# Loads, hashes and splits of the first two head pairs put in another order, and a ranking with its offset summed by TensorE

## The chip, the cores and the metric

The kernel runs on one core of one Trainium2 chip. Its engines are TensorE (PE; its weight loads stand apart as PEld), VectorE (DVE), ScalarE (ACT), GpSimd (POOL) and SyncE (SP), which here only issues DMAs. The metric is the device time of one execution in microseconds, and less is better. Before the change the median of three executions was 389.96 us (389.85 to 390.24).

## The reference

Two stages follow one another. The first is attention on 4 batches of 8 heads, 768 positions of 64 numbers, in which a query sees only keys of its own hash bucket; the bucket is the six signs of a projection.

```python
q_bits = (np.einsum('bhsd,dk->bhsk', q, proj) > 0).astype(np.int64)
q_bucket = np.sum(q_bits * powers, axis=-1)           # k likewise
mask = q_bucket[:, :, :, None] == k_bucket[:, :, None, :]
scores = np.where(mask, scale * np.matmul(q, k.transpose(0, 1, 3, 2)), -1000000000.0)
attn = softmax(scores)                                # + 1e-9 in the divisor
return np.matmul(attn, v)
```

The second takes each batch's 768 x 512 result x, scores each token with `x @ w_gate`, picks the 128 best tokens and adds to them the output of a two-layer ReLU network (512 to 1024 to 512), times the sigmoid of the score.

## The kernel before

**Units.** A head is the unit. Heads are counted 0 to 31; all but head 0 come in pairs that share one load X (128 partitions: two heads of 64 numbers, 768 positions), once for queries (r = 0) and once for keys (r = 1). Head 0 has its own load, Xa, in four pieces, and its own code (the functions with `first` in their names). Exact products are made from two 16-bit parts: a high part that ScalarE rounds (`split_xh`, L495) and a low part, the rest, by VectorE (`split_xl`, L502). V is split the same way (L550, L556).

**What a head needs.** Its projected signs are hashed on TensorE (L463), turned into bits of weight 2^13 on VectorE (`signs`, L480), and its parts and bits are copied to their partitions by DMAs of SP: tile A holds bits and high parts, tile B the low parts (`place_*`, L509). Then come:

- the row maxima over the keys of the same bucket: 6 blocks of two matmuls (`max_unit`, L671), for each a ReLU on ScalarE (tile me, L679) and a reduction on VectorE (tile mj, L688), which gives M. M is turned and put back into A as one more row. A trick halves the columns: the first matmul takes the difference of two halves (`k_diff` L661/L663, `diff_first`);
- nine score blocks of 512 columns (`st_unit`, L722 and L726, tile st) and their exponentials on ScalarE (`st_exp`, L740/L742, tile P);
- the rest R of each exponential beyond bf16, by VectorE (L757) or, for some chunks, by GpSimd (L760), and the product with V (`av`, L776);
- reciprocals and products on VectorE (`recip`, `norm`).

**Beside it.** Weights of the network are loaded and split (`weights`); scores of the finished heads are summed on VectorE (`score`, L813: part 0 over the first 256 columns, part 1 over the rest); batches 0 to 2 are ranked and run through the network while later heads compute (`choose`, `apply_expert`, `expert_steps`). Batch 3 is ranked last (`rank_last`): a token's rank is a count of larger scores, made by VectorE's comparisons (`compare`) and by TensorE's sums of columns (`count`); `pick` makes 128 x 128 selection matrices sel from the ranks, and TensorE uses them to gather (L1177).

**What sets the order.** Every step is an event with a number; the table ORDER says in which sequence the 2676 steps are written down, and each engine executes its own instructions in that sequence, waiting for what its operands need. SP's DMAs are a queue too. PSUM banks are handed out in the order of the table (four for maxima and odd jobs, three for st, one for av), and tiles with a tag have a fixed number of buffers. `mine` remembers a VectorE instruction and `turn` makes the next GpSimd operation wait for it, so that the two do not work on SBUF at once. `keep_warm` writes matmuls of ones into a spare bank (tile wq, L311); nobody reads them.

Of the kernel before, what the change touches and what calls it, by code (L numbers as in the profile page):

```python
# [20 lines left out]
P = 128  # L21
# [222 lines left out]
def body(ctx, tc, qk, v, pj, wg, w1, w2, cst, out):  # L244
# [92 lines left out]
    w1l = cp.tile([P, 4, FF], BF16, name="w1l")  # L337
    w2h = cp.tile([P, 8, DM], F16, name="w2h")
    w2l = cp.tile([P, 8, DM], BF16, name="w2l")

    def load_consts():
        nc.sync.dma_start(cs, cst)

# [3 lines left out]
    def make_ident():  # L347
        nc.scalar.copy(ident16, ident)
# [780 lines left out]
    def rank_last(b):  # L1129
# [39 lines left out]
        for t in range(NC):  # L1169
            pick(sel, t, rank)  # L1170
# [197 lines left out]
```

## Time and profile before

| | |
|---|---|
| median of three executions | 389.96 us |
| profiled execution | 389.61 us |
| its span (first to last instruction) | 387.5 us |
| around the span | 2.11 us |
| busy share PE / DVE / ACT / POOL | 97 / 89 / 81 / 47% |
| granted TensorE clock, mean | 0.99 |

Busy shares are means over the whole span. In the page's 40 slices PE has 6, 8 and 8 tenths in the first three and 9 or more from the fourth to the last but one. [...] A row of a timeline is: start in us, time in us, engine, line, operation, output<-input, shapes, and in brackets how long the engine had been idle and what ended that. [...]

### The profile page before, as it was taken

What the parts mean: (1) busy time and instruction counts of PE and PEld (TensorE: products, weight loads), DVE (VectorE), ACT (ScalarE), POOL (GpSimd) and SP (SyncE); (2) the same over time, 40 slices, a digit from 0 to 9 for tenths busy, and PEclk for the clock granted to TensorE, in tenths of its full rate; (3) what the DMA queues carried; (4) which work ended last, traced back from release to release, by engine and by line L of the source; (5) the groups of instructions that cost most, each with busy time, mean ns of one, the idle gap of its engine ahead of it and who ended that gap; (6) DMA issues with size and microseconds to landing.
All of it is one profiled execution on the core that took longest, in us unless ns stands there. A gap on an engine that the chain in (4) does not pass through costs nothing.

```text
span 387.5 us, 14129 instructions
## 1 busy us (share of the span) xinstructions
PE 374.8 (97%) x5728; PEld 272.6 (70%) x5738; DVE 345.9 (89%) x935; ACT 313.3 (81%) x665; POOL 181.2 (47%) x103
## 2 busy tenths in 40 slices
PE   6889999999999999999999999999999999999995
PEld 4346777677676777687657877667677788778794
DVE  3889999999899989999999999999999999999842
ACT  7899999899998988988588888988988995774210
POOL 8135567474647275655335362545236352630113
PEclk9799999999999999999999999999999999999999
DMA  7568677677776475565855552756463524010301
GB/s 243 148 193 232 172 199 232 169 203 177 223 209 181 100 214 125 140 188 150 208 136 157 135 155 61 217 161 177 100 178 103 113 58 125 6 38 3 110 29 56
DMA packets 26353, 56.37 MB, mean 145 GB/s; under 512 B 4218, under 2 KB 10942, under 8 KB 26288
## 3 DMA queue, kind: packets, MB, share of 16 engines
q1 hardware_dynamic: 15936, 36.92, 36.6%
q10 hardware_dynamic: 9680, 16.45, 13.5%
q0 software_dynamic: 672, 2.10, 1.7%
q8 instruction: 45, 0.74, 0.8%
q14 instruction: 20, 0.16, 0.2%
HBM read 26.58 MB, written 7.35 MB: 88 GB/s over the span
## 4 chain that ended last, share of the span: by engine, by line
PE 78%; issue 7%; ACT 5%; DVE 5%; DMA 2%; POOL 1%; POOLq 0%; SPq 0%; ACTq 0%; DVEq 0%
PE av L776 24%; PE bank L671 14%; PE st L722 14%; PE st L726 14%; PE bank L463 3%; PE bank L995 3%; PE bank L1019 2%; DMA A<-sg 2%; DVE R L757 2%; ACT me L679 1%; ACT P L740 1%; DMA Xa<-in_qk_dram 1%; DVE mj L688 1%; DVE jks L813 1%; PE bank L598 1%
## 5 line engine op out<-in xcount | busy, mean ns | idle before, releaser
L760 POOL TENSOR_TENSOR R<-P 128x1536 f16<-128x1536 f32 x46 | 133.8, 2910 | 134.4 <-DVE V L556 21.1
L776 PEld LDWEIGHTS <-P 128*128 128x128 bf16 x2304 | 125.8, 98 | 26.7 <-issue 1.3
L776 PE MATMUL av<-V,P 128*128 128x65 f16 (+2 forms) x2304 | 133.3, 193 | 0.1
L776 PE MATMUL av<-V,R 128*128 128x65 f16 (+1 forms) x1152 | 126.4, 193 | 0.0
L740 ACT ACTIVATE P<-st 128x512 f32<-128x512 f32 x192 | 111.9, 598 | 17.7 <-PE av L776 9.7
L722 PE MATMUL st<-A 128*128 128x512 f16 (+1 forms) x384 | 119.3, 326 | 1.4 <-ACT P L740 1.2
L726 PE MATMUL st<-B 128*128 128x512 f16 (+1 forms) x384 | 118.6, 326 | 0.7 <-ACT B L432 0.7
L688 DVE CUSTOM_DVE_ANT_0 mj<-bank,me 128x384 bf16<-128x384 f32 x192 | 102.2, 550 | 15.6 <-ACT me L679 7.4
L671 PE MATMUL bank<-A 128*128 128x384 f16 x384 | 108.4, 329 | 3.8 <-DVE A L410 1.0
L776 PEld LDWEIGHTS <-R 128*128 128x128 f16 x1152 | 105.9, 97 | 0.1
L679 ACT ACTIVATE me<-bank 128x384 f32<-128x384 f32 x192 | 92.4, 491 | 14.8 <-PE bank L671 5.7
L757 DVE TENSOR_TENSOR R<-P 128x768 f16<-128x768 f32 x100 | 96.8, 987 | 0.4 <-ACT P L740 0.2
L742 ACT ACTIVATE P<-st 128x512 f32<-128x512 f32 x96 | 56.9, 596 | 2.2 <-PE st L726 0.7
L671 PEld LDWEIGHTS <-A 128*128 128x128 f16 x384 | 34.8, 98 | 23.1 <-issue 4.8
L726 PEld LDWEIGHTS <-B 128*128 128x128 f16 x384 | 37.5, 98 | 18.0 <-issue 2.5
L722 PEld LDWEIGHTS <-A 128*128 128x128 f16 x384 | 37.4, 97 | 15.8 <-issue 2.5
L502 DVE SCALAR_TENSOR_TENSOR T<-X,T 128x768 f16<-128x768 f32 x32 | 31.4, 992 | 0.0
L495 ACT ACTIVATE T<-X 128x768 f16<-128x768 f32 x32 | 26.6, 841 | 0.4 <-DMA B<-T 0.4
L837 POOL TENSOR_TENSOR w1l<-W,w1h 128x512 bf16<-128x512 f32 x8 | 12.8, 1604 | 13.6 <-DVE M L688 4.9
L837 POOL TENSOR_TENSOR w2l<-W,w2h 128x512 bf16<-128x512 f32 x8 | 12.3, 1545 | 12.5 <-DVE R L757 4.0
L798 DVE TENSOR_TENSOR x<-av,rc 128x384 f32<-128x384 f32 x32 | 17.7, 553 | 0.2
L995 PEld LDWEIGHTS <-w1h 128*128 128x128 f16 x256 | 15.9, 98 | 2.1
(137 smaller groups left out, 409.5 us busy)
## 6 DMA issues: line engine op xcount, KB each, us to landing
X<-in_qk_dram SPq DMA_DIRECT2D x32, 384.0 KB
B<-T SPq DMA_DIRECT2D x62, 192.0 KB
A<-T SPq DMA_DIRECT2D x31, 240.0 KB
V<-in_v_dram ACTq DMA_DIRECT2D x16, 384.0 KB
out_dram<-x ACTq DMA_DIRECT2D x6, 768.0 KB
W<-in_w_dram ACTq DMA_DIRECT2D x8, 512.0 KB
sbc<-scores SPq DMA_DIRECT2D x3, 384.0 KB
A<-sg SPq DMA_DIRECT2D x31, 31.5 KB
```

Of the source, the lines that this page charges most:

```text
L502: mine(nc.vector.scalar_tensor_tensor(t[:, o : o + S], st["X", p, r], XS, t[:, i : i + S], op0=ALU.mult, op1=ALU.subtract))
L671: nc.tensor.matmul(pt[:, :384], a[0][:, t * P : (t + 1) * P], a[1][:, 384:768] if i else K[h % NA], start=True, stop=True,)
L679: nc.scalar.activation(me, st["mx", h, t, 0][:, :384], AF.Relu)
L688: nc.vector.tensor_tensor_reduce(out=jk, in0=st["mx", h, t, 1][:, :384], in1=st["me", h, t], op0=ALU.add, op1=ALU.max, scale=1.0 / MS, sca ...
L722: nc.tensor.matmul(pt[:, o : o + n], a[1][:, c * P : (c + 1) * P], a[0][:, q0 : q0 + n], start=True, stop=False,)
L726: nc.tensor.matmul(pt[:, o : o + n], bt[:, 0, c * P : (c + 1) * P], bt[:, 1, q0 : q0 + n], start=False, stop=True,)
L740: nc.scalar.activation(pp[:, r, 0:512], pt, AF.Exp, scale=ES)
L742: nc.scalar.activation(pp[:, :, 512:768], pt.rearrange("p (a b) -> p a b", a=2), AF.Exp, scale=ES)
L757: mine(nc.vector.tensor_tensor(t[:, r], pp[:, r], hi_view(pp, r), op=ALU.subtract))
L760: turn(nc.gpsimd.tensor_tensor(t, pp, hi_view(pp, a), op=ALU.subtract))
L776: nc.tensor.matmul(o[:, t, :n], l, vv[:, c, hh, v0 : v0 + n], start=False, stop=last and l is lo, skip_group_check=True,)
L995: nc.tensor.matmul(hp[:, f * P : (f + 1) * P], w[:, k, o : o + P], x[:, k * P : (k + 1) * P], start=(f == 0 and k == 0 and i == order[0]), ...
```

## The change

Six things change.

- **Loads.** In the first microseconds SP loads only head 0 (Xa), pair 0 (X0_0, X0_1) and the 128 x 128 identity. V0, X1_1 and X1_0 get a wait for VectorE's last sign instruction of head 0 (`gate`). The rest of the constants (`cs`) also has it and stands later. V0 is issued by SP and no longer by ScalarE.
- **Hashes of pairs 0 and 1.** They were hashed together, each half of the columns in one PSUM bank. Now each pair has its bank, 64 partitions of it used twice (`hash_pair`), and `sign_pair` makes two sign instructions and one difference per pair on VectorE. Before, the difference of this first group was GpSimd's.
- **High parts.** X0_1's and X1_0's are made by GpSimd (`tensor_scalar`) instead of ScalarE. The 16-bit identity is cast by VectorE instead of ScalarE.
- **Order.** The first 300 events of ORDER stand in another sequence; some 25 of the later ones move by a few places, at most some dozen (steps of `choose` and `apply`, a `split_xl` and a `max_red`). Two `keep_warm` of eight matmuls each move from within head 0's maxima to within head 2's.
- **Scores.** Part 1's instructions are remembered by `mine`, so the GpSimd operation written next waits for them.
- **Ranking.** For batch 3 `behind` adds one matmul of the identity with six columns of constants to the count, and sel is then made by one comparison instead of a subtraction and a comparison.

```diff
--- before.py
+++ after.py
@@ -53,160 +53,160 @@
 ORDER = (
-    0, 142, 288, 289, 20, 15, 1, 16, 11, 21, 72, 144, 7, 75, 83, 141, 77, 10, 76, 85, 6, 71, 24, 12,
...
+    0, 10, 20, 9, 6, 142, 144, 146, 143, 59, 1, 21, 27, 15, 16, 3, 17, 18, 7, 72, 74, 76, 73, 12,
...
@@ -338,14 +338,17 @@
     w2h = cp.tile([P, 8, DM], F16, name="w2h")
     w2l = cp.tile([P, 8, DM], BF16, name="w2l")
 
+    def load_ident():
+        nc.sync.dma_start(cs[:, :P], cst[:, :P])
+
     def load_consts():
-        nc.sync.dma_start(cs, cst)
+        behind_of(nc.sync.dma_start(cs[:, P:], cst[:, P:]), "gate", "load")
 
     def load_gate():
         nc.scalar.dma_start(wgt, wg)
 
     def make_ident():
-        nc.scalar.copy(ident16, ident)
+        nc.vector.tensor_copy(ident16, ident)
 
     def make_consts():
         nc.vector.tensor_copy(iota16, iota)
@@ -359,13 +362,17 @@
     def mine(i):
         st["port"] = i
 
+    def behind_of(i, key, why):
+        if key in st:
+            tc.add_manual_dep(
+                getattr(i, "ins", i), getattr(st[key], "ins", st[key]).name,
+                mybir.DependencyInfo(mybir.DependencyClass.Sync, mybir.DependencyReason.SCHED_ONLY),
+                reason=why,
+            )
+
     def turn(i):
-        if TURNS and "port" in st:
-            tc.add_manual_dep(
-                getattr(i, "ins", i), getattr(st["port"], "ins", st["port"]).name,
-                mybir.DependencyInfo(mybir.DependencyClass.Sync, mybir.DependencyReason.SCHED_ONLY),
-                reason="port",
-            )
+        if TURNS:
+            behind_of(i, "port", "port")
 
     def need(*keys):
 
@@ -375,12 +382,16 @@
 
     def load_x(p, r):
         x = sb.tile([P, S], F32, tag="X", name=f"X{p}_{r}", bufs=XB)
-        nc.sync.dma_start(x, qk[p, r])
+        i = nc.sync.dma_start(x, qk[p, r])
+        if p == 1:
+            behind_of(i, "gate", "load")
         st["X", p, r] = x
 
     def load_v(pr):
         t = sb.tile([P, NC, 2, D], F32, tag="V", name=f"V{pr}", bufs=1)
-        (nc.scalar if ACT_V else nc.sync).dma_start(t, v[pr])
+        i = (nc.scalar if pr else nc.sync).dma_start(t, v[pr])
+        if not pr:
+            behind_of(i, "gate", "load")
         st["V", pr] = t
 
     def negate():
@@ -407,7 +418,7 @@
         j, n = 32 * (2 * e + r), 2 * NB + 2
         x, y = st["hpa", r, e][j : j + n, :384], A[0][r][0:n, e * 384 : (e + 1) * 384]
         if r:
-            nc.vector.tensor_scalar(
+            st["gate"] = nc.vector.tensor_scalar(
                 y, x, pjt[j : j + n, 64:65], pjt[j : j + n, 65:66], op0=ALU.is_gt, op1=ALU.mult
             )
         else:
@@ -454,6 +465,32 @@
         nc.scalar.copy(A[0][0][0:1, t0 * P : t1 * P], pt[0:1, :n])
         pmax.give(f"mt0_{e}")
         st[("row1", 0) if e else ("row", 0)] = True
+
+    def hash_pair(p):
+        hp = st["hpp", p] = pmax.take(f"hpp{p}")
+        for e in range(2):
+            for r in range(2):
+                i = 64 * e + 32 * r
+                nc.tensor.matmul(
+                    hp[i : i + 32, :384], pjt[:, 0:32], st["X", p, r][:, e * 384 : (e + 1) * 384],
+                    start=True, stop=True, tile_position=(0, i),
+                )
+
+    def sign_pair(p):
+        if ("sg", 0) not in st:
+            st["sg", 0] = sb.tile([P, S // 2 + S], F16, tag="sg", name="sg0", bufs=2)
+        w = slice(64 * p, 64 * p + 64)
+        hp, t = st["hpp", p], st["sg", 0][w]
+        sd, sg = t[:, : S // 2], t[:, S // 2 :]
+        for e in range(2):
+            i = slice(64 * e, 64 * e + 64)
+            nc.vector.tensor_scalar(
+                sg[:, e * 384 : (e + 1) * 384], hp[i, :384], pjt[i, 66:67], pjt[i, 67:68],
+                op0=ALU.is_gt, op1=ALU.mult,
+            )
+            st["sgd", p, e] = True
+        pmax.give(f"hpp{p}")
+        mine(nc.vector.tensor_tensor(sd, sg[:, 0:384], sg[:, 384:768], op=ALU.subtract))
 
     def hash_half(g, e):
         hp = pmax.take(f"hp{g}_{e}")
@@ -483,16 +520,16 @@
         )
         pmax.give(f"hp{g}_{e}")
         if e:
-            if g:
-                mine(nc.vector.tensor_tensor(sd, sg[:, 0:384], sg[:, 384:768], op=ALU.subtract))
-            else:
-                nc.gpsimd.tensor_tensor(sd, sg[:, 0:384], sg[:, 384:768], op=ALU.subtract)
+            mine(nc.vector.tensor_tensor(sd, sg[:, 0:384], sg[:, 384:768], op=ALU.subtract))
 
     def split_xh(p, r):
         if ("T", p) not in st:
             st["T", p] = sb.tile([P, TW], F16, tag="T", name=f"T{p}", bufs=TB)
         o = KH if r else QH
-        nc.scalar.activation(st["T", p][:, o : o + S], st["X", p, r], AF.Copy, scale=XS)
+        if (p, r) not in {(0,1),(1,0)}:
+            nc.scalar.activation(st["T", p][:, o : o + S], st["X", p, r], AF.Copy, scale=XS)
+        else:
+            nc.gpsimd.tensor_scalar(st["T", p][:, o : o + S], st["X", p, r], XS, None, op0=ALU.mult)
         st["XH", p, r] = True
 
     def split_xl(p, r):
@@ -810,12 +847,14 @@
         for t in range(t0, t1):
             st["scd", b, part, t] = True
             jk = sb.tile([P, 384], BF16, tag="jks", name=f"jks{b}_{part}_{t}", bufs=2)
-            nc.vector.tensor_tensor_reduce(
+            i = nc.vector.tensor_tensor_reduce(
                 out=jk[:, : d1 - d0], in0=x[:, t, d0:d1], in1=wgt[:, d0:d1],
                 op0=ALU.mult, op1=ALU.add, scale=1.0,
                 scalar=st["sc", b, part - 1][:, t : t + 1] if part else 0.0,
                 accum_out=sc[:, t : t + 1],
             )
+            if part:
+                mine(i)
 
 
     def load_w(i):
@@ -861,10 +900,15 @@
             op1=ALU.mult, accum_out=cnt[:, i : i + 1],
         ))
 
-    def count(i, cm, rp):
+    def behind(rp):
+        nc.tensor.matmul(
+            rp[:, :NC], ident, cs[:, 3 * P + NC : 3 * P + 2 * NC], start=True, stop=False, skip_group_check=True
+        )
+
+    def count(i, cm, rp, first=True):
         for j in range(i, NC):
             nc.tensor.matmul(
-                rp[:, j : j + 1], cm[:, j], oneb[:, 0:1], start=(i == j == NC - 1), stop=(i == 0),
+                rp[:, j : j + 1], cm[:, j], oneb[:, 0:1], start=first and i == j == NC - 1, stop=(i == 0),
                 skip_group_check=True,
             )
 
@@ -1151,6 +1195,7 @@
                     bp[:, j0 * P : j1 * P],
                 )
         rp = st_bank(f"rp{b}")
+        behind(rp)
         yield
         cnt = sb.tile([P, NC], F32, tag="cnt", name=f"cnt{b}", bufs=1)
         cms = {}
@@ -1159,15 +1204,15 @@
             compare(i, sc, sbc, cms[i], cnt)
             yield
             if i < NC - 1:
-                count(i + 1, cms[i + 1], rp)
+                count(i + 1, cms[i + 1], rp, False)
                 yield
-        count(0, cms[0], rp)
+        count(0, cms[0], rp, False)
         yield
         rank = sb.tile([P, NC], F32, tag="rank", name=f"rank{b}", bufs=1)
         nc.vector.tensor_tensor(rank, rp[:, :NC], cnt, op=ALU.subtract)
         sel = sb.tile([P, NC, P], F16, tag="T", name=f"sel{b}", bufs=TB)
         for t in range(NC):
-            pick(sel, t, rank)
+            nc.vector.tensor_scalar(sel[:, t], iota16, rank[:, t : t + 1], None, op0=ALU.is_equal)
         yield
         need(*(("xsl", k) for k in range(4)))
         xs, xps = st["xs"], [mx_bank(f"xp{b}_{r}") for r in range(2)]
@@ -1240,10 +1285,14 @@
     at(low_first, 0)
     for i, n in enumerate(WARM[2:]):
         at(keep_warm, 2 + i, n)
-    for g in range(NH // 4):
+    for p in range(2):
+        at(hash_pair, p)
+        at(sign_pair, p)
+    for g in range(1, NH // 4):
         for e in range(2):
             at(hash_half, g, e)
             at(signs, g, e)
+    at(load_ident)
     for fn in (score_v, score_vh, score_vl):
         at(fn)
     for k in range(4):
```

Numbers behind a name in the rows that follow are the head or pair, the part and the buffer: `X0_1` is pair 0's keys, `me0_3` the ReLU of head 0's block 3, `T0` pair 0's high and low parts, `sg0` the signs of pairs 0 and 1.

On ACT, from the end of Xa's high parts on, there stands before:

```order
L415 ACTIVATE s00_170<-bank0_64,pjt_75 14x384
L416 ACTIVATE A0_90<-s00_170,pjt_75 14x384
L415 ACTIVATE s01_175<-bank2_66,pjt_75 14x384
L416 ACTIVATE A0_90<-s01_175,pjt_75 14x384
L495 ACTIVATE T0_182<-X0_1_163 128x768
L679 ACTIVATE me0_1_189<-bank0_64 128x384
L679 ACTIVATE me0_3_194<-bank2_66 128x384
L679 ACTIVATE me0_0_228<-bank0_64 128x384
L383 DMA V0_230<-in_v_dram 128x768
L495 ACTIVATE T1_235<-X1_0_165 128x768
L495 ACTIVATE T1_235<-X1_1_167 128x768
L495 ACTIVATE T0_182<-X0_0_187 128x768
```

and with the change:

```order
L530 ACTIVATE T0_185<-X0_0_183 128x768
L426 ACTIVATE s00_198<-bank0_64,pjt_75 14x384
L427 ACTIVATE A0_90<-s00_198,pjt_75 14x384
L426 ACTIVATE s01_201<-bank2_66,pjt_75 14x384
L427 ACTIVATE A0_90<-s01_201,pjt_75 14x384
L443 ACTIVATE B0_94<-Xa_105 64x768
L716 ACTIVATE me0_0_209<-bank3_67 128x384
L716 ACTIVATE me0_1_216<-bank0_64 128x384
L443 ACTIVATE B0_94<-Xa_105 128x768
L716 ACTIVATE me0_2_237<-bank0_64 128x384
L716 ACTIVATE me0_3_240<-bank1_65 128x384
L587 ACTIVATE V0_96<-V0_214 128x12x64
```

X0_0's high part now stands ahead of head 0's signs, and head 0's two parts of B (L443) among its first maxima; X0_1's, X1_0's and the identity's casts are gone, X1_1's stands five rows below the end of the piece, and the load of V0 has left this queue.

On DVE, from the first instruction that waits for Xa, there stands before:

```order
L438 SCALAR_TENSOR_TENSOR B0_94<-Xa_105,A0_90 64x768
L410 TENSOR_SCALAR A0_90<-bank1_65,pjt_75 14x384
L410 TENSOR_SCALAR A0_90<-bank3_67,pjt_75 14x384
L422 TENSOR_TENSOR A0_90<-A0_90 128x384
L688 ISA mj0_1_225,M0_84<-bank3_67,me0_1_189 128x384
L688 ISA M0_84 128x1
L688 ISA mj0_3_232,M0_84<-bank2_66,me0_3_194 128x384
L688 ISA M0_84 128x1
L688 ISA mj0_0_252,M0_84<-bank1_65,me0_0_228 128x384
L688 ISA M0_84 128x1
```

and with the change:

```order
L449 SCALAR_TENSOR_TENSOR B0_94<-Xa_105,A0_90 64x768
L421 TENSOR_SCALAR A0_90<-bank1_65,pjt_75 14x384
L539 SCALAR_TENSOR_TENSOR T0_185<-X0_0_183,T0_185 128x768
L421 TENSOR_SCALAR A0_90<-bank3_67,pjt_75 14x384
L351 CAST ident16_87<-cs_74 128x128
L433 TENSOR_TENSOR A0_90<-A0_90 128x384
L487 TENSOR_SCALAR sg0_219<-bank1_65,pjt_75 64x384 x2
L493 TENSOR_TENSOR sg0_219<-sg0_219 64x384
L725 ISA mj0_0_223,M0_84<-bank2_66,me0_0_209 128x384
L725 ISA M0_84 128x1
```

X0_0's low part now stands between the two sign instructions of head 0 (L421), the second of which is the gate; the identity and pair 0's signs and difference follow ahead of the first reduction.

On SP, behind the first two loads, there stands before:

```order
L378 DMA X0_1_163<-in_qk_dram 128x768
L378 DMA X1_0_165<-in_qk_dram 128x768
L378 DMA X1_1_167<-in_qk_dram 128x768
L378 DMA X0_0_187<-in_qk_dram 128x768
L302 DMA Xa_105<-in_qk_dram 64x768
L342 DMA cs_74<-in_cst_dram 128x397
L302 DMA Xa_105<-in_qk_dram 64x768
L509 DMA A1_91<-T0_182 64x1920
L378 DMA X2_1_262<-in_qk_dram 128x768
L509 DMA A1_91<-sg0_260 14x1152
L509 DMA A1_91<-sg0_260 14x768
```

and with the change:

```order
L385 DMA X0_0_183<-in_qk_dram 128x768
L385 DMA X0_1_188<-in_qk_dram 128x768
L342 DMA cs_74<-in_cst_dram 128x128
L302 DMA Xa_105<-in_qk_dram 64x768 x2
L392 DMA V0_214<-in_v_dram 128x768
L385 DMA X1_1_229<-in_qk_dram 128x768
L385 DMA X1_0_232<-in_qk_dram 128x768
L546 DMA A1_91<-T0_185 64x1920
L546 DMA A1_91<-sg0_219 14x1152
L546 DMA A1_91<-sg0_219 14x768
L546 DMA A2_92<-T0_185 64x1920
```

Pair 0 and the identity come first and Xa's upper halves right behind them; V0, X1_1 and X1_0 stand behind these and ahead of the first copy to A1, and the wait of the gate is V0's.

## Rows read from the trace of the kernel before

**Rows 1.** Stretches: us, busy us and count per engine, PE clock, DMA share, GB/s.

```profile
8.00:15.70 7.70, 6.90 (x43) 2.85 (x43) 4.77 (x13) 6.62 (x13) 2.96 (x4) 0.56 0.74 192
15.70:20.00 4.30, 3.09 (x18) 1.23 (x17) 4.30 (x8) 3.69 (x8) 0.24 (x1) 1.00 0.49 144
20.00:24.00 4.00, 2.96 (x17) 1.53 (x16) 3.27 (x12) 3.47 (x9) 1.03 (x1) 1.00 0.95 273
24.00:28.00 4.00, 3.73 (x35) 1.96 (x34) 3.46 (x12) 4.00 (x11) 2.18 (x2) 1.00 0.54 150
28.00:46.00 18.00, 17.92 (x293) 12.62 (x292) 17.25 (x43) 17.65 (x39) 10.59 (x6) 1.00 0.68 192
46.00:360.00 314.00, 311.69 (x4994) 228.94 (x4999) 296.33 (x807) 268.19 (x574) 151.26 (x61) 1.00 0.53 145
```

**Rows 2.** Chain of waits, first 60 us: start us, us, what ended last.

```profile
0.75 3.28 DMA Xa<-in_qk_dram
...
9.99 0.85 PE wq L311 x8
...
11.49 2.71 PE bank L463 x16
...
39.91 1.43 PE bank L463 x16
```

**Rows 3.** Timeline of ACT, first 20 us: start us, us, line, tiles.

```profile
4.05 1.59 ACT L392 ACTIVATE A<-Xa 64x768 f16<-64x768 f32 x2 [1.11 <-DMA Xa<-in_qk_dram]
5.76 0.57 ACT L415 ACTIVATE s<-bank,pjt 14x384 f32<-14x384 f32 x1
...
7.60 0.61 ACT L416 ACTIVATE A<-s,pjt 14x384 f16<-14x384 f32 x1
...
8.97 0.87 ACT L679 ACTIVATE me<-bank 128x384 f32<-128x384 f32 x2
...
10.69 2.31 ACT L495 ACTIVATE T<-X 128x768 f16<-128x768 f32 x3
...
18.22 0.60 ACT L740 ACTIVATE P<-st 128x512 f32<-128x512 f32 x1 [0.48 <-PE st L726]
```

**Rows 4.** Timeline of DVE, first 20 us.

```profile
4.92 0.95 DVE L438 SCALAR_TENSOR_TENSOR B<-Xa,A 64x768 f16<-64x768 f32 x1 [3.02 <-ACT A L392]
5.91 1.39 DVE L410 TENSOR_SCALAR A<-bank,pjt 14x384 f16<-14x384 f32 x2
...
15.34 1.41 DVE L438 SCALAR_TENSOR_TENSOR B<-Xa,B 64x768 f16<-64x768 f32 x1
```

**Rows 5.** Groups by line and form: count, busy us, mean ns.

```profile
L760 POOL TENSOR_TENSOR R<-P 128x1536 f16<-128x1536 f32 x46 | 133.8, 2910 | 134.4 <-DVE V L556 21.1 <-DVE R L757 20.3 <-ACT me L679 12.6
...
L837 POOL TENSOR_TENSOR w1l<-W,w1h 128x512 bf16<-128x512 f32 x8 | 12.8, 1604 | 13.6 <-DVE M L688 4.9 <-ACT w1h L835 2.5 <-ACT me L679 1.9
...
L480 DVE TENSOR_SCALAR sg<-bank,pjt 128x384 f16<-128x384 f32 x16 | 10.5, 672 | 0.8 <-PE bank L463 0.6
...
L813 DVE CUSTOM_DVE_ANT_0 jks<-x,wgt,sc 128x256 bf16<-128x256 f32 x18 | 7.7, 477 | 0.0
...
L661 DVE TENSOR_TENSOR T<-T 128x384 f16<-128x384 f16 x15 | 5.7, 381 | 0.0
```

**Rows 6.** Timeline, first 20 us: the DMA queue of SP, POOL and PE.

```profile
1.81 2.12 SPq L378 DMA_DIRECT2D X<-in_qk_dram  x4
...
15.03 0.91 POOL L489 TENSOR_TENSOR sg<-sg 128x384 f16<-128x384 f16 x1 [4.59 <-DVE sg L480]
...
15.97 1.77 SPq L509 DMA_DIRECT2D A<-sg  x2
...
19.14 0.65 PE L671 MATMUL bank<-A 128*128 128x384 f16 x3 [0.22 <-DMA A<-sg]
```

**Rows 7.** Timeline of the last ranking, 365 to 372 us.

```profile
367.89 1.43 DVE L874 TENSOR_SCALAR sel<-iota,cs,rank 128x128 f16<-128x128 f16 x6
...
368.79 2.84 PE L1177 MATMUL bank<-sel,xs 128*128 128x128 f16 x48
```

306 rows, old and new, of the table ORDER are left out of this document.

## The prediction, made before the changed kernel had run

> **What bounds the kernel now.** I read four views, in this order: the busy slices of the page, the table by stretches, the chain of waits of the first 60 us, and the timelines of ACT and DVE there. In the slices the reader is to see that PE is full from the fourth slice on. The stretches put numbers to it [rows 1]: from 28 to 46 us PE is idle for 0.08 of 18 us and from 46 to 360 us for 2.3 of 314. What is gained there must be PE's own work, and the change takes none away. Before 28 us it is another kernel: from 15.7 to 24 us PE idles 1.21 + 1.04 = 2.25 us, and from 8 to 15.7 us it has 43 matmuls, at a clock of 0.56. There the chain runs through the first loads, ACT and DVE. ACT idles 1.08 + 0.61 + 0.53 = 2.22 us between 8 and 24 us, DVE 2.93 + 0 + 0.73 + 0.54 = 4.20 us between 8 and 28 [rows 1]. The first exponential, from which all heads follow, starts at 18.22 us [rows 3]. So the question is how much sooner the start hands a full queue to PE, and whether ACT and DVE, 85% and 94% busy in the long stretch (268.19 and 296.33 of 314), can then keep that lead.
>
> **Loads and head 0.** A load lands 3.28 us after its issue when nothing is ahead of it [rows 2]. SP issues four X from 1.81 us in 2.12 us, 0.53 each [rows 6]. X0_0 now has the first of these places, behind Xa's pieces, and I put its landing at 6.4 us: 1.81 + 3.28, and 1.3 for the bytes ahead of it (an estimate; 5.1 without them is the lower bound). On ACT it stands ahead of head 0's signs. ACT ends Xa's high parts at 4.05 + 1.59 = 5.64 us [rows 3], waits 0.75 us, and splits X0_0 in 0.77 us (three in 2.31 [rows 3]), to 7.2. The four sign instructions took from 5.76 to 8.21 us, 2.45 in all [rows 3], and now end at 9.6. DVE does X0_0's low part (0.95, as the 768 columns of B [rows 4]) between its two signs (1.39 for two [rows 4]): it starts when ACT has the high part, at 7.2, and the gate falls at 7.2 + 0.95 + 0.70, about 8.9, instead of 5.91 + 1.39 = 7.3. Both engines' bits, which the maxima need, are there 1.4 to 1.6 us later than before.
>
> It is made good in what follows. On ACT from 9.6, with 0.77 us for each cast of 768 columns and 0.87 for two me [rows 3]: one part of B to 10.4, me0_0 and me0_1 to 11.2, the other part of B to 12.0, two me to 12.9, V0's high part to 13.6 (V0 is issued at 8.9 and lands by 12.3 if it takes the 3.28; cover 0.6 us), the issue of a weight load, at SP's 0.53, to 14.2, two me to 15.0, the row's cast, at a sign's 0.6, to 15.6, X1_1's high part to 16.4. Nothing in this list waits for a landing later than 12.3 or for GpSimd. The first exponential then starts at 16.2 to 16.6 us, against 18.22: 1.6 to 2.0 us sooner, and I take **1.8**. Head 1's tile A is sooner too: its signs are on DVE by 11.2 us; two such copies are 1.77 us of SP's time, and PE waited for the second until 19.14, 3.2 after their first issue at 15.97 [rows 6]; that gives 14.4 now, ahead of need.
>
> **GpSimd's two high parts.** No row has a GpSimd operation of this form. From below: R's pace, 2910 ns for 1536 columns, is 1.9 ns a column, 1.46 us for 768, and with one input less perhaps half, 0.75; from above: w1l's pace, 1604 ns for 512, gives 2.4 us [rows 5]. I take 1.5. X0_1's starts at about 7.5 us, when X0_1 has landed one place behind X0_0, and feeds a difference, head 1's tile A and a low part that DVE reaches at 12.2; even 2.4 us is hidden. X1_0's has from 14 to 20 us. ACT loses 2 x 0.77 = 1.54 us of work and the identity's cast, 0.13 or more at the same pace per column: about 1.7.
>
> [...]
>
> **Sign work on DVE.** A sign instruction costs by its columns and not its partitions: 0.70 us for 14 partitions [rows 4], 0.672 for 128 [rows 5]. Two become four for pairs 0 and 1, +1.34 us; two differences come from GpSimd, 2 x 0.38 [rows 5] = 0.76; the identity's cast is some 0.15. DVE has **2.25 us more** to do before head 1 is through. It has 4.20 us of idle time to put it in. By the steps above I see it wait 1.3 us (for the first me, between the reductions, for X1_1), so its lead is 4.20 - 2.25 - 1.3 = 0.6; with as much waiting as before it is -2.25, with none 1.95. ACT's lead is 1.7 + 2.22 less the new wait for X0_0 (0.75) and one for the first score block (0.4): 2.8. PE's is the 1.8. PE keeps it as far as the other two feed it. DVE lags PE by 1.2, and its 6% of slack return that in some 20 us, so I charge only a part: **+0.2** (0 to 1.2).
>
> **Clock and warm-up.** At 8 to 15.7 us the clock was 0.56, and the hash of the pairs took 2.71 us where the same sixteen matmul records took 1.43 later [rows 2]. In the change pair 0's hash fills PE while it waits for signs, and pair 1's runs among score blocks. [...] I take **+0.2**.
>
> **Scores and ranking.** The mark on the 18 score instructions of batches 0 to 2 can delay the next GpSimd operation by those still to run, 0.477 us each [rows 5], three at a time at most: 0 to 1.4 us, six times. GpSimd is busy 151.26 of 314 us [rows 1] and R has four buffers, so this costs nothing, or gains some contention: -0.3 to +0.3, I take 0. In the last ranking the selection (six in 1.43 us) runs at 367.89 us beside PE's own queue, and PE gathers from 368.79 without waiting [rows 7]; shortening it gives nothing. The added matmul stands in a full PE: 0 to 0.3, **+0.1**.
>
> **Sum.** -1.8 + 0.2 + 0.2 + 0.1 = -1.3 us. The profiled execution took 389.61, 387.5 of span and 2.11 around it, which stay; so 388.3. The median lies 0.35 above that execution, which gives 388.7 (389.96 - 1.3).
>
> **Rivals.**
> 1. *ACT's lead passes whole.* DVE catches up beside PE-full stretches, and 2.8 less 0.3 (warm-up and matmul) arrive: 387.5. For it: every wait of the list is covered. Against: DVE, with 94%, is the fuller engine.
> 2. *DVE takes the bound.* Its 0.6 less the same 0.3 is all that arrives: 389.7, no change that can be told. For it: 2.25 us more work in the very stretch where DVE idles 0.00 of 4.30 [rows 1].
> 3. *Slower: the clock stays low.* PE is nearly idle at 8.3 to 9.6 us and thin up to 15.7. [...] For it: the clock was 0.56 with more matmuls in that stretch; against: the score blocks come sooner and dense. [...]
> 4. *Slower: GpSimd's rests come late.* If two of the six waits for scores reach PE with 0.9 us each: 390.5.
>
> **How the numbers follow.** Chances: forecast 0.42 (388.0 to 389.2), rival 1 0.16, rival 2 0.23, rival 3 0.14, rival 4 0.05. A measurement of this kernel can tell 0.2%, 0.78 us, from no change. Faster by more: the forecast, rival 1 and a little of 2, 0.60. Within: the rest of 2 and the mild ends of 3 and 4, 0.25. Slower: 0.15. The range that leaves out 2 in 10 reaches from rival 1's better half, 387.2, to near rival 3, 390.6.
>
> **What would show it.** Right: the first exponential at 16.2 to 16.6 us; PE idle under 1 us from 16 to 24 us; GpSimd's splits near 1.5 us with no one waiting; the same head's blocks at 46 us of before some 1.3 us sooner, and that distance kept to the end. Wrong: clock below 1.00 after 20 us; ACT or SP idle for V0 or X1_1; DVE without idle time and PE waiting for reductions from 24 to 40 us; the distance lost between 46 and 360 us.

## The result and the profile after

Slower: 393.06 us in the median of four executions (391.75 to 393.98) against 389.90 (389.64 to 390.24), a ratio of 1.0081, 95% interval 1.0061 to 1.0101, or 3.2 us. Forecast were 388.7 us and a range from 387.2 to 390.6. The profiled execution took 391.75 us, 389.7 of span. It is the fastest of the four: its 2.2 us of longer span are followed here step by step, the other 1 us only by the runs.

First its stretches, in the columns of [rows 1].

```profile
8.00:15.70 7.70, 5.64 (x24) 1.91 (x23) 7.08 (x17) 6.93 (x13) 3.60 (x3) 0.72 0.73 224
15.70:20.00 4.30, 4.07 (x12) 1.27 (x10) 2.78 (x6) 2.96 (x6) 1.83 (x1) 0.50 0.95 260
20.00:24.00 4.00, 4.00 (x41) 2.10 (x38) 2.89 (x8) 3.31 (x8) 0.01 (x1) 0.90 0.62 142
24.00:28.00 4.00, 4.00 (x51) 2.48 (x44) 3.65 (x12) 3.95 (x11) 3.94 (x3) 1.00 0.71 276
28.00:46.00 18.00, 17.40 (x255) 11.50 (x253) 17.90 (x45) 16.96 (x37) 9.31 (x6) 1.00 0.54 144
46.00:360.00 314.00, 311.66 (x4981) 228.28 (x4979) 296.39 (x803) 269.82 (x576) 152.21 (x61) 1.00 0.53 146
```

From 15.7 to 20 us the clock is 0.50 where it was 1.00, VectorE idles 1.52 us where it idled 0.00, and the DMA engines are 95% busy instead of 49%. From 20 to 28 us TensorE is full, where it had 1.04 + 0.27 us of idle time before. Next ScalarE's timeline: X0_0's high part, the first exponential, and the cast of head 1's row of maxima (mr), which the prediction did not look at.

```profile
6.60 0.84 ACT L530 ACTIVATE T<-X 128x768 f16<-128x768 f32 x1
...
17.12 0.60 ACT L777 ACTIVATE P<-st 128x512 f32<-128x512 f32 x1 [0.35 <-PE st L763]
...
27.33 0.24 ACT L740 CAST mr<-bank 6x128 f16<-6x128 f32 x1
```

The first exponential is 1.1 us sooner than in [rows 3]. The cast of head 1's row is later; in the kernel before it stands here:

```profile
26.20 0.24 ACT L703 CAST mr<-bank 6x128 f16<-6x128 f32 x1
```

So a lead of 1.1 us has become a lag of 1.1 within 10 us. What lies between, from the chain of waits and the timelines of TensorE and VectorE:

```profile
13.18 4.83 DMA A<-sg
...
21.22 0.78 PE bank L474 x8
```
```profile
18.15 1.44 PE L708 MATMUL bank<-A 128*128 128x384 f16 x4 [0.21 <-DMA A<-sg]
...
21.15 0.85 PE L474 MATMUL bank<-X,pjt 128*32 128x384 f32 x8
...
25.71 0.49 PE L708 MATMUL bank<-A 128*128 128x384 f16 x2
```
```profile
20.20 0.56 DVE L725 CUSTOM_DVE_ANT_0 mj<-bank,me 128x384 bf16<-128x384 f32 x1 [1.55 <-ACT me L716]
...
22.07 1.37 DVE L487 TENSOR_SCALAR sg<-bank,pjt 64x384 f16<-64x384 f32 x2 [0.82 <-PE bank L474]
...
26.18 0.56 DVE L725 CUSTOM_DVE_ANT_0 mj<-bank,me 128x384 bf16<-128x384 f32 x1
```

Head 1's second copy of signs is issued at 13.18 and lands at 18.01; 14.4 was forecast. Its maxima then start 1 us sooner than in [rows 6], and among them stand pair 1's hash and signs. GpSimd's high parts took 2.26 us each on average (below: count, busy us, mean ns), near the upper bound of 2.4. No engine waited for them directly; but GpSimd makes a difference behind the first of them (L700), and SP waited 1.0 us for that with the copy of T to tile A, behind which the copies of signs stand. The tail gathers 2.22 us later than [rows 7], 0.17 of it its own: sel takes 1.07 instead of 1.43 us but starts later, behind the added matmul.

```profile
L532 POOL TENSOR_SCALAR T<-X 128x768 f16<-128x768 f32 x2 | 4.5, 2261 | 4.4 <-DMA X<-in_qk_dram 4.4
```
```profile
371.01 2.84 PE L1222 MATMUL bank<-sel,xs 128*128 128x128 f16 x48
```

### The profile page after: what moved, and what is told of

It reads as the page before. It is cut to its first block, busy times and chain, and to the rows that moved or that the text cites. A ratio compares the mean times of both kernels' runs of the same rounds, so it can differ in the third digit from the quotient of the medians.

```text
span 389.7 us, 14157 instructions
## 1 busy us (share of the span) xinstructions
PE 377.2 (97%) x5740; PEld 273.0 (70%) x5740; DVE 348.4 (89%) x940; ACT 312.9 (80%) x662; POOL 183.5 (47%) x104
## 3 DMA queue, kind: packets, MB, share of 16 engines
q10 hardware_dynamic: 9536, 16.06, 12.6%
## 4 chain that ended last, share of the span: by engine, by line
PE 74%; DVE 8%; issue 7%; DMA 5%; ACT 4%; POOL 1%; SPq 0%; POOLq 0%; DVEq 0%; ACTq 0%
PE av L813 23%; PE st L759 14%; PE bank L708 14%; PE st L763 13%; PE bank L1039 3%; DMA A<-sg 3%; DVE R L794 2%; PE bank L1063 2%; PE bank L500 2%; ACT me L716 1%; DMA Xa<-in_qk_dram 1%; DVE mj L725 1%; DVE jks L850 1%; PE bank L635 1%; ACT P L777 1%
## 5 line engine op out<-in xcount | busy, mean ns | idle before, releaser
L708 PE MATMUL bank<-A 128*128 128x384 f16 x384 | 107.3, 330 | 3.7 <-DVE M L725 1.5
L530 ACT ACTIVATE T<-X 128x768 f16<-128x768 f32 x30 | 25.0, 839 | 0.3 <-DMA B<-T 0.3
L876 POOL TENSOR_TENSOR w1l<-W,w1h 128x512 bf16<-128x512 f32 x8 | 11.7, 1464 | 15.5 <-ACT P L777 7.2
```

Source lines behind the costliest of these rows:

```text
L708: nc.tensor.matmul(pt[:, :384], a[0][:, t * P : (t + 1) * P], a[1][:, 384:768] if i else K[h % NA], start=True, stop=True,)
```

## Experiments

Theories. **A**: VectorE, empty at 18 to 22 us and full from 26 to 42, sets the pace. **B**: TensorE's clock, low at 14 to 23 us, does (B' adds: at another time in each execution). **C**: loads that the gate puts off delay head 1's copies. **D**: the 25 later moves of the order cost by themselves. Each kernel was timed beside the kernel before; ratios carry 95% intervals of some 0.002, so two variants can be told apart from about 1 us on. What lies below 1 us is read from one trace of each, which shows places. Edits of ORDER, which holds only numbers, are given by the names of the steps. The places (us): first exponential, first and last reduction of head 1, its row, head 3's first exponential, the last reciprocals, and when the clock was 0.50 after 7 us (the last microseconds left out).

| | exp | first | last | row | head 3 | recip | clock 0.50 |
|---|---|---|---|---|---|---|---|
| before | 18.22 | 21.55 | 25.04 | 26.20 | 50.67 | 359.97 | 7.9-14.7 |
| after | 17.12 | 20.20 | 26.18 | 27.33 | 51.80 | 362.01 | 7.1-10.6, 14.0-20.8 |
| start_only | 16.50 | 20.16 | 25.32 | 26.48 | 50.94 | 364.03 | 211.5-214.9 |
| late_order | 17.02 | 21.00 | 27.52 | 28.68 | 53.13 | 362.06 | 16.0-22.8 |
| copies_first | 17.21 | 20.66 | 25.69 | 26.74 | 51.39 | 361.58 | 11.1-17.9 |
| gate_off | 17.14 | 19.85 | 25.15 | 26.30 | 50.76 | 361.14 | 15.7-19.1 |
| warm_throughout | 16.49 | 20.54 | 25.70 | 26.85 | 51.65 | 364.25 | none |
| warm_half_signs | 15.82 | 20.74 | 25.90 | 27.05 | 51.99 | 365.07 | none |
| all_mended | 16.47 | 19.18 | 25.54 | 26.59 | 51.61 | 361.18 | none |
| late_moves_only | 18.10 | 21.47 | 24.96 | 26.12 | 50.58 | 363.56 | 7.4-14.3 |
| vector_load | 18.48 | 21.75 | 26.53 | 27.41 | 54.19 | 364.33 | 8.8-15.6 |

**The ranking and the mark, each alone** on the kernel before.

```diff
+        behind(rp)
-            pick(sel, t, rank)
+            nc.vector.tensor_scalar(sel[:, t], iota16, rank[:, t : t + 1], None, op0=ALU.is_equal)
```


> The kernel before with the change to the last ranking alone (one matmul of offsets, one comparison per selection). Theory A (the loss comes from the start of the kernel, where VectorE runs out of slack): 390.0, no difference that can be told, since the selection ran beside a queue of PE. Rival (a part of the loss lies at the end: the added matmul stands in a full PE and delays the gather): 390.3 to 391.


```diff
+            if part:
+                mine(i)
```


> The kernel before with the mark on the score instructions alone: the GpSimd operation written next waits for them. Theory A: 390.0, no difference. Rival (the 0.9 us by which the changed kernel falls back between 46 and 360 us come from GpSimd's rests waiting for scores): 390.6 to 391.

390.23 us, ratio 0.9999 (0.9986 to 1.0012), and 390.21, 0.9996 (0.9981 to 1.0011). Neither costs anything that can be told.

**The rest alone**: the change without these two.

> The changed kernel without its marks on scores and without its ranking: loads, hashes, high parts and order alone. Theory A: nearly the whole loss stays, 392 to 393.2. Rival (marks and ranking make it): 389 to 390.

395.76 us, 1.0141 (1.0119 to 1.0164): more than the whole change, which neither theory said. The trace shows two things. In it the clock never fell in the first 200 us, the first exponential came at 16.50, within the forecast of 16.2 to 16.6, and head 1's row still at 26.48. Here are, in the columns of [rows 1], the stretches from the start of head 1's first matmul of maxima to the start of its last, for the kernel before, after and start_only:

```profile
19.14:24.52 5.38, 4.34 (x25) 2.42 (x26) 4.49 (x14) 4.73 (x12) 1.55 (x1) 1.00 0.95 274
18.15:25.71 7.56, 7.56 (x54) 3.74 (x54) 4.79 (x14) 6.10 (x15) 1.72 (x1) 0.83 0.78 212
18.57:24.85 6.28, 6.28 (x54) 3.39 (x54) 4.29 (x13) 5.43 (x14) 1.69 (x1) 1.00 0.81 205
```

With the new order TensorE has no idle time there. At the same clock of 1.00 it works 6.28 us instead of 4.34, and the stretch lasts 0.90 us longer. The other thing stands at 207 us, on VectorE and GpSimd:

```profile
206.33 0.48 DVE L850 CUSTOM_DVE_ANT_0 jks<-x,wgt,sc 128x256 bf16<-128x256 f32 x1
206.74 0.09 DVE L850 DVE_READ_ACCUMULATOR2_ANT sc<- 128x1 f32 x1
206.74 2.96 DVE L850 CUSTOM_DVE_ANT_0 jks<-x,wgt,sc 128x256 bf16<-128x256 f32 x1
```
```profile
206.40 3.02 POOL L797 TENSOR_TENSOR R<-P 128x1536 f16<-128x1536 f32 x1 [2.85 <-ACT P L777]
```

A score instruction written behind the start of a rest took 2.96 us instead of 0.48: it ends at 209.70, just behind the rest's end at 209.42. Why the one waits for the other, no run shows. The mark prevents just this: in the trace after, the marked score instructions take 0.48 us at most and the others 0.70.

**The later moves**, put into the kernel before, and taken out of the changed one.

```diff
 ORDER = (          # by named steps
-    first 300 and later steps of one kernel
+    first 300 of one, later steps of the other
```


> The kernel before with the 25 later moves of the changed order alone (steps of ranking, network and splits, a few places each). Theory D (these moves cost by themselves, which late_order's trace suggests: the changed kernels fall back 0.65 to 1.4 us between 50 us and the end, with the old late order they gain 0.4 to 0.8): 390.6 to 391.3 beside 390.0. Rival (only the shifted alignment of GpSimd and VectorE after another start costs it): 390.0.

> The changed kernel with the steps of its order behind the first 301 in the sequence of the kernel before (the 25 moves of a few places undone). Theory D (the 0.8 us lost at 196 to 216 us come from a step of batch 0's network that now stands behind a wait for the hash of a pair): 0.4 to 0.9 us less than the changed kernel, 392.2 to 392.7 beside 390.0. Rival: the loss there comes from the shifted alignment of GpSimd and VectorE and stays: 393.1.

393.16 us, 1.0099 (1.0065 to 1.0132), and 390.77, 1.0012 (0.9989 to 1.0035). The times say D, at more than its price. Alone, the moves bring the collision just shown, at 206.80 us with 2.96 us, so most of their 3.1 us is that. In the changed kernel, whose mark prevents it, they cost otherwise: batch 0's result (ye) now stands behind a sign instruction that waits for TensorE,

```profile
201.55 0.68 DVE L517 TENSOR_SCALAR sg<-bank,pjt 128x384 f16<-128x384 f32 x1 [0.89 <-PE bank L500]
202.14 0.74 DVE L1072 SCALAR_TENSOR_TENSOR ye<-bank,ss,xe 128x512 f32<-128x512 f32 x1
```

where before it ran ahead of it:

```profile
199.56 0.75 DVE L1028 SCALAR_TENSOR_TENSOR ye<-bank,ss,xe 128x512 f32<-128x512 f32 x1
200.57 0.68 DVE L480 TENSOR_SCALAR sg<-bank,pjt 128x384 f16<-128x384 f32 x1 [0.26 <-PE bank L463]
```

From head 17's to head 19's first exponential, around this place, it is 18.62 us before and 18.74 in late_order, but 19.47 after, 19.46 in copies_first and 19.48 in gate_off: the step costs 0.8 us. From head 3's first exponential to the last reciprocals the traces with the moves fall back by 0.9 (after), 0.9 (copies_first) and 1.1 (gate_off); late_order gains 0.4.

**Copies and gate.**

```diff
+place_signs(1)   # then load_x(1, 1), load_x(1, 0); load_x(2, 1) behind place_signs(2)
-weights          # first load: from head 0's maxima to behind max_red(1, 4)
```


> The changed kernel with the first weight load and the loads of X1_1, X1_0 and X2_1 behind the copies for head 1 in the queues; X1_1's high and low parts stand a little later. The copies then have no load of 384 or 512 KB ahead of them. Theory C (head 1's second copy took 4.83 us, from 13.18 to 18.01, because of those loads, and TensorE and VectorE starved for it): the copy lands at about 15.5 to 16, head 1's first maxima start 2 us sooner, VectorE's wait of 1.55 us at 18.7 goes, and 0.5 to 1.5 us come back, 391.6 to 392.6. Theory A without C: the same idle time appears elsewhere, 393.1.


```diff
-        if p == 1:
-            behind_of(i, "gate", "load")
-        if not pr:
-            behind_of(i, "gate", "load")
```


> The changed kernel with V0's, X1_1's and X1_0's wait for the gate taken away (the order of the queue stays): the three loads are issued right behind Xa's upper halves at 4.6 to 6 us instead of at 9.2 to 10.5. Theory C (the loads that the gate puts off stand in the DMA queues ahead of head 1's copies and are what starves TensorE and VectorE from 16 to 20 us): the second copy for head 1 lands at 15.5 to 16.5 us instead of 18.0, and 0.7 to 1.5 us come back, 391.6 to 392.4 beside a kernel before of 390.0. Rival (the first weight load at 13.0 us alone stands ahead of the copies): it lands at 17.5 to 18, 393.

391.45 us, 1.0048 (1.0031 to 1.0065), and 390.40, 1.0014 (0.9995 to 1.0033). In copies_first C holds: the copy for head 1 lands at 15.3 us instead of 18.0, and 1.3 us come back, as forecast. Without the gate it lands at 17.4, near the place that the rival gave, and 2.6 us come back, more than C forecast; so that this gain comes through the copies is not shown. Head 1's row is no sooner than before in either: the copies end a wait, and the reductions still need 5.0 and 5.3 us, against 3.5 before.

**Clock.** Warm-up matmuls back among head 0's maxima, and (with the old late order) in each of TensorE's waits from 9 to 18 us.

```diff
+max_unit(0, 3, 1)  # then keep_warm(2, 8); keep_warm(3, 8) ahead of st_unit(0, 3)
```


> The changed kernel with its two groups of eight warm-up matmuls moved from head 2's maxima to head 0's: one behind block 3's second matmul, one ahead of the first score block. Theory B (the clock of 0.50 from 14.0 to 20.9 us costs): the clock is back sooner in most executions, the first exponential at 16.5 instead of 17.1 us, and about 0.9 us come back, 392.2. Theory A alone: VectorE's backlog stays and takes most of it, 392.6 to 393.1.


```diff
+keep_warm: 8 behind hash_pair(0), 8 behind max_unit(0, 3, 1), 16 behind max_unit(0, 4, 0), 24 behind st_unit(0, 4)
```


> late_order with warm-up matmuls in each of TensorE's waits from 9 to 18 us: 8 behind pair 0's hash, 8 and 16 within head 0's maxima, 24 ahead of head 1's first maxima (those in head 2's maxima are gone). Theory B' (the clock's fall between 14 and 23 us, at another time in each execution, costs 0.9 to 2.2 us at 50 us): the clock stays at 1.00 from 10 to 24 us in most executions, the distance at 50 us is about +0.3 as in the trace of start_only, 389.7 to 390.4, and the times spread over 1 us instead of 3.8. Rival: as late_order, 390.8 with its spread.

391.71 us, 1.0049 (1.0027 to 1.0072), and 390.59, 1.0016 (0.9997 to 1.0035). The first is 1.2 us less than 1.0081, just clear of noise, where B said 0.9; its profiled execution, 393.50 us, had the clock down from 20.0 to 23.5 and does not show how. In warm_throughout the clock stayed up and the row came at 26.85; late_order, the same but for the warm-ups, had 28.68 with the clock down from 16.0 to 22.8. So the clock is 1.8 us there, and about 0.9 in the trace after (27.33 against start_only's 26.48). Its time did not fall below late_order's, and why is open. The profiled execution, 393.95 us, is the slowest of twelve: a T subtraction took 2.77 us in it, beside a rest at 89.7 us.

The mean granted clock of every execution is on record, and in some of these runs it goes with the time, while in the kernel before it does not. All four executions of the changed kernel had 0.986 or 0.987. In gate_off the two with as low a clock took 392.06 and 392.22 us, the ten others 388.61 to 391.75. In late_order the nine at 0.991 or below have a median of 391.23, the three at 0.996 or above took 389.51 to 390.07; the kernel before, timed beside it, has 390.38 for the sixteen at 0.991 or below and 390.99 for the six at 0.997 or above (one of 2148.79 us left out). So a part of what these two runs give back may be the clock.

**VectorE.** Work moved, given to GpSimd, added and left out. low_early:

```diff
+split_xl(1, 0)     # behind split_vl(0) instead of behind r_chunk(0, 5)
```


> The changed kernel with one VectorE instruction moved: the low part of X1_0 (0.95 us) stands behind V0's low part instead of behind head 0's rests, that is at about 18.7 us, where VectorE waited 1.55 us, instead of at 32.3 us, where it has no idle time. Theory A (VectorE is empty at 18 to 22 us and full from 26 to 42 us, and the backlog sets the pace): 0.5 to 0.95 us less than the changed kernel, 392.1 to 392.6. Rival B (TensorE's clock and late copies set it, VectorE only follows): no difference, 393.1.

392.04 us, 1.0060 (1.0038 to 1.0082): 0.8 us less than 1.0081, as A says; but the intervals overlap, so B's "no difference" is not excluded.

```diff
-        mine(nc.vector.tensor_tensor(sd, sg[:, 0:384], sg[:, 384:768], op=ALU.subtract))
+        nc.gpsimd.tensor_tensor(sd, sg[:, 0:384], sg[:, 384:768], op=ALU.subtract)
```


> The changed kernel with the two differences of pairs 0 and 1 on GpSimd and the identity's cast on ScalarE: some 0.9 us less work on VectorE. Theory A: up to 0.9 us less, 392.2 to 392.8, most of it from pair 1's difference, which stands at 23.5 us where the backlog begins. Rival B: 393.1, or more if the copies of head 1's signs wait for GpSimd.


```diff
-        if g not in POOL_R[h % 2 + (h == NH - 1)]:
+        if g not in (POOL_R[h % 2 + (h == NH - 1)] if h else (1, 2)):
```


> The changed kernel with head 0's rests of chunks 4 and 5 as one GpSimd operation (2.75 us, where GpSimd waits from 30.7 to 33.4 us) instead of two VectorE ones (1.84 us at 30.6 us). Theory A (VectorE's backlog between 26 and 42 us sets the pace): 1.0 to 1.7 us less than the changed kernel, 391.4 to 392.1 beside a kernel before of 390.0. Rival B (clock and copies alone): no difference, 393.1, or more where VectorE's two-input work runs beside GpSimd.

394.16 us, 1.0113 (1.0089 to 1.0137), and 394.37, 1.0100 (1.0060 to 1.0141): both worse than forecast. In the second VectorE's load from 28 to 36 us fell to 4.89 of 8, GpSimd's rose to 7.87, and TensorE, busy for 6.59, waited for it. So work taken from VectorE did not help here: the other engine was later.

```diff
+        for i in (slice(0, 64), slice(64, P)):   # per half, and the difference on VectorE
```


> The kernel before, with its own loads and order, but with the sign work of the changed kernel: the first group's two sign instructions are four of 64 partitions, its difference is two instructions on VectorE instead of one on GpSimd, and VectorE casts the identity. About 2.2 us more on VectorE at 13 to 16 us. Theory A (VectorE has no slack left in the first 45 us): 391 to 392. Rival (late copies and the low clock of TensorE lose the time, VectorE's work is covered by its idle time): 389.7 to 390.4.


```diff
+        nc.vector.tensor_tensor(jx, t[:, 0:384], t[:, 384:768], op=ALU.subtract)   # six times
```


> The kernel before with six more VectorE subtractions of 384 columns (0.36 us each, 2.2 us in all) between 24 and 32 us; nobody reads them. It does the work of the reference and 2.2 us of idle work beside it. VectorE idles some 0.9 us from 24 to 46 us there. Theory A (VectorE sets the pace from 24 to 46 us): 1.0 to 1.5 us more, 391.0 to 391.5 beside 390.0. Rival (TensorE does, VectorE has slack by its lead): 390.0 to 390.3.


```diff
-        for e in range(2):
+        for e in range(1):   # and no difference
```


> warm_throughout with half of the sign work of pairs 0 and 1 left out: one sign instruction per pair instead of two, and no difference (zeros by GpSimd stand there): 2.1 us less for VectorE. Its buckets are others than the reference's. Theory A (VectorE's extra 2.25 us take the start's gain): the gain of 1.7 us at the first exponential comes through, 388.2 to 389.3. Rival (the order of the first heads' work takes it, whatever VectorE has to do): as warm_throughout, within 0.3 us.

392.39 us, 1.0051 (1.0033 to 1.0070); 393.46, 1.0085 (1.0065 to 1.0105); 393.27, 1.0057 (1.0027 to 1.0087). The first two say that VectorE's work before 33 us is on the path of the kernel before: TensorE, nearly full in [rows 1], idles in vector_load:

```profile
24.00:28.00 4.00, 2.52 (x27) 1.42 (x27) 4.00 (x12) 3.12 (x9) 1.92 (x1) 1.00 0.64 185
28.00:36.00 8.00, 6.04 (x85) 3.97 (x84) 7.78 (x17) 6.28 (x14) 2.81 (x2) 1.00 0.62 184
```

The 2.2 us added became 3.5 at head 3 since two of the six took 1.66 and 1.31 us beside GpSimd. The third speaks against VectorE as what took the lead of the change: in the traces 2.1 us less sign work left head 1's last reduction at 25.90 (25.70 with it), and the time is 1.6 us above warm_throughout's, hardly clear of noise, which neither theory forecast. Its profiled execution, 395.05 us, has a T subtraction of 2.77 us too; where the 1.6 us come from is open.

**Put together.** The old late order, no gate, the weight load and X2_1 behind the copies, low_early, and warm-ups at 9 and 13 us. Two mixtures with the gate left in came first. The late order, copies_first and low_early together gave 392.48 us, 1.0043 (1.0022 to 1.0064); 390.3 was forecast if the three add up and 391.4 if they share one loss. It is 1.2 us worse than the late order alone, which no run explains. With the warm-ups among head 0's maxima as well it was 391.07 us, 1.0012 (0.9994 to 1.0029), where 389.0 to 389.5 was forecast if the clock costs by itself and 390 to 391 if VectorE takes it back.

> The changed kernel with what the runs pointed to: the old late order, no gate, the first weight load and X2_1 behind the copies for head 1, X1_0's low part behind V0's, and the warm-up matmuls at 9 and 13 us. If the copies, the late moves and the clock are the loss: the copies land at 15 us, the distance at 50 us is -0.5 to -1.0, and the time 388.8 to 389.6, better than both kernels. If the sign work on VectorE takes the start's gain all the same: 390.0 to 390.6.

389.20 us, 0.9976 (0.9957 to 0.9994): better than both kernels, by 0.9 us against the one before. Its profiled execution, 390.88 us, lies 1.7 us above the median (all executions: 387.75 to 391.38) and does not show the gain: at head 3 it is 0.9 us later than before (51.61 against 50.67), where 0.5 to 1.0 sooner was forecast. It shows a copy landing at 15.2, VectorE busy for 4.27 of the 4.30 us up to 20, and then TensorE idle for 1.57 of 4 us:

```profile
15.70:20.00 4.30, 3.63 (x24) 1.65 (x24) 4.27 (x10) 3.80 (x9) 0.00 (x0) 1.00 0.75 190
20.00:24.00 4.00, 3.82 (x35) 2.20 (x34) 2.98 (x9) 3.80 (x9) 1.83 (x1) 1.00 0.91 238
24.00:28.00 4.00, 2.43 (x28) 1.40 (x28) 3.29 (x10) 2.88 (x8) 3.83 (x5) 1.00 0.91 291
```

## Why the prediction was wrong

- **"The first exponential, from which all heads follow."** This step failed. 1.8 us were forecast, 1.1 came, 1.7 with the clock up. But the heads follow from head 1's row of maxima: from it to head 3's first exponential it is 24.45 to 24.47 us before, after and in start_only, late_order, gate_off and late_moves_only, and more in the other traces of the table. That row was at 26.20 before and never sooner than 26.30 in any trace with the new start. The new order puts all nine score blocks of head 0, pair 1's hash (0.78 us of the chain) and V's sums (0.28) ahead of head 1's last maximum; seven blocks stood there before, and neither of these among head 1's maxima. Two blocks of 0.43 (one from 25.28 to 25.71 us in the trace after, at a clock of 1.00), the hash and the sums make the 1.9 us by which TensorE works longer among these maxima (6.28 against 4.34). Head 0's last exponential starts at 26.11 instead of 29.82, but the reductions of head 1 last from 20.20 to 26.18 instead of 21.55 to 25.04. The lead was spent on head 0. With earlier copies, less sign work or a high clock that last reduction came at 25.15 to 25.90 us in the traces of the table, behind the 25.04 of before; that another order of these blocks would bring it sooner is argued and was not tried by itself.
- **Pair 1's hash "among score blocks"** was priced at nothing. Before, the hashes of both pairs were 2.71 us of the chain at 11.49 us [rows 2], ahead of the first exponential. Now pair 1's stands behind it, in a stretch where TensorE has no idle time: that brings the first exponential forward, and not head 1's row.
- **Head 1's copies, "14.4 now, ahead of need."** The second landed at 18.0: X1_1 and X1_0, put off by the gate, the copy of T and the weight load were in flight when it was issued. The prediction asked where the loads land, not what they stand in front of.
- **Clock.** 0.2 us were taken for it and the warm-ups, a term that no run shows. The trace after shows a clock of 0.50 from 7.1 to 10.6 and from 14.0 to 20.8 us, at which a score block took 0.85 us (19.38 to 20.23) instead of 0.43, and which cost some 0.9 us of the trace; the two groups of warm-ups took 0.45 us each of a full TensorE (26.03 to 26.48 and 27.71 to 28.16). Rival 3, a clock that stays low, had one of the causes.
- **VectorE.** Rival 2 said that VectorE takes the gain; in the trace it waited instead. 1.3 us of waits were forecast from 8 to 28 us, 0.62 + 1.52 + 1.11 + 0.35 = 3.6 came, the longest (1.55) for head 1's first maxima.
- **The later moves** stood in the description and got no term, without a reason. By the trace they are some 0.9 us of the 2.2, by the times up to 2.7 of 3.2.
- **Right:** GpSimd's splits had no direct waiters, at 2.26 us instead of 1.5; the gate at 9.15 (8.9), V0 by 12.6 (12.3); marks 0; the added matmul 0.17 (0.1) in the trace.

For the profiled execution: 1.1 us by head 3 (0.9 clock, 0.3 the start itself), 0.9 from there to the last reciprocals, 0.2 in the tail. For the median the parts are not settled: no gate gives back 2.6 us and the old late order 2.7, of 3.2, so they share a loss, and the three edits mixed first did not add up. Which collisions the other executions of the changed kernel had, and where their clock was low, was not seen.

## What to carry to other kernels

Measure a lead at the link that lets the next unit start, not at the first visible event: an order can turn it into work done early that nobody waits for. Price a moved step by the stretch it moves into. And a load that is put off does not only land later, it stands in front of what is issued next: among such loads the copy here took 4.83 us, ahead of them about 2.

## What the hardware showed

- Two VectorE instructions that started within a GpSimd rest lasted until just behind its end: in start_only a score instruction for 2.96 us instead of 0.48 (to 209.70, the rest to 209.42), in warm_throughout a subtraction for 2.77 instead of 0.35 (to 92.47, the rest to 92.25). In the trace before the longest of the two kinds were 1.06 and 0.59 us; with the 25 later moves alone a score instruction took 2.96 us at 206.80. Whether this also makes the spread of the executions, 391.75 to 393.98 after and 389.64 to 390.24 before, was not seen.
- A copy of 14 rows took 4.83 us from issue to landing among large loads (13.18 to 18.01 in after), and about 2 where they were behind it (13.15 to 15.2 in all_mended).
- The clock fell at 14.0, 16.0, 15.7 us, or not within the first 200 us, in one execution each of after, late_order, gate_off and start_only, whose starts are nearly the same.
